# Clustered attention and two feed-forward layers on one core: attention per whole head, W from rounded parts, reloads split in place

## The chip, the core and the metric

One Trainium2 chip, of which the program uses one core. The metric is device time in microseconds (us). The engines are TensorE (PE in the views; its weight loads are PEld), VectorE (DVE), ScalarE (ACT), GpSimd (POOL, idle here but for a few set-up instructions) and SyncE (SP), whose queue issues every DMA of this kernel.

## The reference

```python
q_n, k_n, c_n = normalised q, k, centroids
q_assign = argmax(q_n . c_n); k_assign = argmax(k_n . c_n)   # 16 clusters per head
scores = where(q_assign == k_assign, q @ k.T / 8, -1e9)
attn = exp(scores - max) / (sum + 1e-9);  x = attn @ v        # B=2, H=8, S=768, D=64
x = x as [1536 tokens, 512]
h = x @ w_in                                                  # 512 -> 2048
g = (a0 + a1 h + a2 h^2 + a3 h^3) / (1 + |b0||h| + |b1| h^2 + 1e-6)
y = g @ w_out                                                 # 2048 -> 512
out = ((y @ w1) * (y @ w2)) @ w3 @ w_out2                     # 512 -> 1024 -> 1024 -> 512
```

The weights arrive as 64-bit words, which the kernel decodes to float32 itself.

## The kernel before

**The work.** The 1536 tokens are four chunks of 384 (c = 0 to 3; two per batch). For each chunk there are four stages of matmuls, each of blocks of one 128 x 1024 weight tile: p1 (w_in, 8 blocks, and the rational function on 128 x 768 values behind each), p2 (w_out, 8 blocks), p3 (w1 and w2 together, 8 blocks, and the product of the two), p4 (W, 4 blocks). W is w3 @ w_out2, made once at the start: `FirstW` makes four of its eight row tiles in one go from 16 half blocks, `w_block` one more each for m = 4 to 7.

**Attention.** It goes by chunk: `Attn(c)` works on the 384 queries of a chunk, and per head on three units of 128 queries. A unit is a score matmul (L802), a maximum (DVE, L814), an exponential (ACT, L815), six transposes in two lots (L842) that ScalarE copies out (L845). After two heads `av` multiplies by v (L876). K is rounded and split for the first chunk of a batch, stored to `k_d`, and loaded again for the second chunk.

**Numbers in two parts.** A float32 product is made in one of two ways. A block of kind "D" multiplies plain float32 words (L545). The others split weight and activation each into a rounded part (fp32r, a copy on ScalarE, `hi`) and the rest (a subtraction on VectorE, `lo`), and add three products hi.hi, hi.lo, lo.hi (L547 to L549). In chunk 0 the w_in and w_out blocks are of kind "D" and the w1/w2 blocks of kind "E" (decoded, then split); all are also stored to DRAM as decoded words. Later chunks reload them, kind "S": the load lands in a slot of the class `raw`, is rounded into `hi` (L501) and subtracted into `lo` (L502), two slots of the class `w`. p4 loads both parts of W ready made, kind "L". W itself is made from plain float32 words (L590, L606).

**Order.** All operations are written down as tasks with their operands, and a planner (`Plan`) places them on the four queues by list scheduling with fixed costs, going forward and backward some rounds; the best order is emitted as it stands. Each engine runs its instructions strictly in that order. Buffers are slots of classes (`SLOTS`: six `w`, three `raw`, three `et`, two PSUM slots each of `s` for scores and p1, `t` for transposes and attention output, `m` for the other stages). `CFG` holds the numbers that steer the priorities: in which window of blocks how much attention lies (`AT`), and leads and offsets.

Of the kernel before, what the change touches and what calls it, by code (L numbers as in the profile page):

```python
# [21 lines left out]
    F0=('in', 'out'),  # L22
    KEEP=(),
    NORM=(4, 4, 4, 4),
    NW=(1, 4),
    AT=(1.5, 2.2083, 2.5833, 4.0, 4.0, 4.0, 4.0, 4.0, 4.0),
    M1=1,
    LEAD=(5.9, 35.7, 45.3),
    ALEAD=(23.9, 20.0),
    MLEAD=252.0,  # L30
    AOFF=3.7,
    SLOTS={'w': 6, 'raw': 3, 'y': 3, 'x': 2, 'ab': 4, 'x2': 2, 'g': 16, 'et': 3, 'E': 4, 'kqr': 1, 'A': 2, 'B': 2, 'v': 1, 'sm': 6, 'nn': 3, 's': 2, 't': 2, 'm': 2, 'sums': 2, 'rb': 1},
    WO2=-768.4,
# [254 lines left out]
def kernel(  # L288
# [15 lines left out]
    cfg=CFG,  # L304
# [17 lines left out]
    if not only_plan:  # L322
# [67 lines left out]
    def masks(b, pr):  # L390
# [11 lines left out]
        def one(which, src):  # L402
# [19 lines left out]
            op("ACT", 0.83, lambda: s.activation(two(rn.t), ss.t[:, :, 0:TC], AF.Ln, bias=tiny), [ss], [rn], p0)  # L422
# [3 lines left out]
            op("DVE", 0.87, lambda: w.tensor_tensor(two(u.t), two(rn.t), lg.t[:, :, 0:TC], ALU.mult), [rn, lg], [u], p0)  # L426
# [6 lines left out]
            def count():  # L433
                for hf in range(2):
                    nc.tensor.matmul(cnt.t[:, hf, 0:TC], tri, u.t[:, hf * TC:(hf + 1) * TC])
# [3 lines left out]
                two(v.t), cnt.t[:, :, 0:TC], 0.0, two(u.t), ALU.is_equal, ALU.mult), [cnt, u], [v], p0)  # L439
            if which:  # L440
                op("ACT", 0.74, lambda: s.activation(u.t, v.t, AF.Copy, scale=-BIG), [v], [u], p0)
                dma(lambda: msk_d[b, :, 0:TC], lambda: u.t[:, 0:TC], 196608, [u], [("msk", b, 1)], p0)
                dma(lambda: msk_d[b, :, TC + S:], lambda: u.t[:, TC:], 196608, [u], [("msk", b, 2)], p0)
            else:
                op("ACT", 0.74, lambda: s.activation(u.t, v.t, AF.Identity, bias=one1, scale=-1.0), [v], [u], p0)
                dma(lambda: msk_d[b, :, TC:TC + S], lambda: u.t, 393216, [u], [("msk", b, 0)], p0)
# [26 lines left out]
    class Blk:  # L473
# [7 lines left out]
        def prep(self):  # L481
            k, at = self.kind, self.at
            pl, psp = at - cfg["LEAD"][0 if k != "L" else 1] - (0 if k == "L" else cfg["LEAD"][1]), at - cfg["LEAD"][1]
            if k in "DE":
                self.f = Buf("w", [P, WB])
                raws = [load_raw(self.src, i, at - cfg["LEAD"][2]) for i in range(2)]
                for i in range(2):
                    decode(raws[i], lambda i=i: self.f.t[:, i * HB:(i + 1) * HB], (self.f, i), psp)
                if self.full is not None:
                    dma(lambda: self.full[0](), lambda: self.f.t, 524288, [(self.f, 0), (self.f, 1)], [self.full[1]], at)  # L490
                if k == "D":
                    return
            elif k == "S":
                self.f = Buf("raw", [P, WB])
                dma(lambda: self.f.t, self.full[0], 524288, [self.full[1]], [(self.f, 0), (self.f, 1)], pl)
            self.hi, self.lo = Buf("w", [P, WB], F32R), Buf("w", [P, WB], F32R)
# [3 lines left out]
            else:  # L500
                op("ACT", 0.95, lambda: nc.scalar.copy(self.hi.t, self.f.t), [(self.f, 0), (self.f, 1)], [self.hi], psp)  # L501
# [14 lines left out]
    def moe_blk(c, n, i, src):  # L516
# [3 lines left out]
        if c == 0:  # L520
            if n in F0:
                return Blk("D", src, full)
# [554 lines left out]
```

## Time and profile before

| what | us |
|---|---|
| median of 3 runs (range) | 808.32 (805.76 to 809.25) |
| the profiled execution's own time | 805.77 |
| its span, first to last instruction | 804.0 |
| PE busy in the span | 775.6 (96%) |
| VectorE, ScalarE busy | 614.1 (76%), 555.8 (69%) |

The difference between time and span (1.8 us) lies outside the instructions. Busy time of PE counts a matmul from its start to its modelled end, and neighbours overlap, so the distance from one start to the next tells more than the mean duration does. The same holds, less strongly, for VectorE and ScalarE.

### The profile page before, as it was taken

What the parts mean: (1) busy time and instruction counts of PE and PEld (TensorE: products, weight loads), DVE (VectorE), ACT (ScalarE), POOL (GpSimd) and SP (SyncE); (2) the same over time, 40 slices, a digit from 0 to 9 for tenths busy, and PEclk for the clock granted to TensorE, in tenths of its full rate; (3) what the DMA queues carried; (4) which work ended last, traced back from release to release, by engine and by line L of the source; (5) the groups of instructions that cost most, each with busy time, mean ns of one, the idle gap of its engine ahead of it and who ended that gap; (6) DMA issues with size and microseconds to landing.
All of it is one profiled execution on the core that took longest, in us unless ns stands there. A gap on an engine that the chain in (4) does not pass through costs nothing.

```text
span 804.0 us, 11696 instructions
## 1 busy us (share of the span) xinstructions
PE 775.6 (96%) x4225; PEld 636.7 (79%) x4225; DVE 614.1 (76%) x842; ACT 555.8 (69%) x959; POOL 0.7 (0%) x6
## 2 busy tenths in 40 slices
PE   3998999998999999999999999999999999999998
PEld 1346655565665768888889889899999999999998
DVE  6988887659999987989999663299994399983440
ACT  4887877778797867899898755378763388663331
POOL 0000000000000000000000000000000000000000
PEclk9999999999999999999999999999999999999999
DMA  8998899998768499666777842243557343653324
GB/s 322 367 304 265 272 293 262 294 284 269 233 174 295 135 368 315 206 207 216 224 234 234 286 161 97 87 132 105 206 199 229 105 134 130 228 178 132 132 103 146
DMA packets 67641, 172.08 MB, mean 214 GB/s; under 512 B 7680, under 2 KB 29952, under 8 KB 67584
## 3 DMA queue, kind: packets, MB, share of 16 engines
q1 hardware_dynamic: 67584, 171.34, 65.2%
q8 instruction: 33, 0.54, 0.3%
q14 instruction: 24, 0.20, 0.1%
HBM read 134.88 MB, written 33.29 MB: 209 GB/s over the span
## 4 chain that ended last, share of the span: by engine, by line
PE 81%; DMA 10%; ACT 4%; DVE 3%; issue 1%; SPq 1%; ACTq 0%; DVEq 0%
PE m L547 12%; PE m L548 12%; PE m L549 12%; PE s L802 6%; PE t L842 6%; PE t L876 6%; PE m L545 5%; DMA raw<-in_w_in_dram 4%; PE s L547 4%; PE s L545 4%; PE s L549 4%; PE s L548 4%; PE m L606 2%; PE t L590 1%; DMA raw<-fin 1%
## 5 line engine op out<-in xcount | busy, mean ns | idle before, releaser
L502 DVE TENSOR_TENSOR w<-raw,w 128x1024 fp32r<-128x1024 f32 x72 | 87.9, 1222 | 60.8 <-ACT w L501 55.2
L501 ACT CAST w<-raw 128x1024 fp32r<-128x1024 f32 x72 | 75.8, 1053 | 82.0 <-PE m L548 59.7
L814 DVE TENSOR_REDUCE sm<-s 128x1 f32<-128x768 f32 x96 | 90.7, 951 | 16.9 <-PE s L802 15.9
L845 ACT COPY et<-t 128x384 f32<-128x384 f32 x192 | 87.8, 494 | 21.6 <-PE t L842 19.5
L815 ACT ACTIVATE E<-s,sm 128x768 f32<-128x768 f32 x96 | 88.2, 920 | 12.5 <-DVE sm L814 10.7
L842 PEld LDWEIGHTS t<-ident,E 128*128 128x128 f32 x576 | 68.8, 140 | 34.1 <-issue 12.1
L842 PE MATMUL t<-ident,E 128*128 128x128 f32 x576 | 86.6, 276 | 7.7 <-ACT et L845 4.4
L547 PE MATMUL m<-x,w 128*128 128x384 f32 x256 | 87.4, 341 | 0.0
L548 PE MATMUL m<-x,w 128*128 128x384 f32 x256 | 86.2, 337 | 0.0
L549 PE MATMUL m<-x,w 128*128 128x384 f32 x256 | 86.1, 336 | 0.0
L876 PE MATMUL t<-et,v 128*64 128x384 f32 x384 | 69.0, 494 | 0.0
L547 PE MATMUL s<-x,w 128*128 128x384 f32 x192 | 66.1, 345 | 0.0
L547 PE MATMUL m<-g,w 128*128 128x384 f32 x192 | 64.9, 338 | 0.0
L549 PE MATMUL s<-x,w 128*128 128x384 f32 x192 | 64.9, 338 | 0.0
L549 PE MATMUL m<-g,w 128*128 128x384 f32 x192 | 64.7, 337 | 0.0
L548 PE MATMUL s<-x,w 128*128 128x384 f32 x192 | 64.6, 336 | 0.0
L548 PE MATMUL m<-g,w 128*128 128x384 f32 x192 | 64.6, 336 | 0.0
L802 PE MATMUL s<-A 128*128 128x384 f32 x192 | 60.6, 397 | 2.4 <-ACT E L815 1.8
L466 ACT ACTIVATE y<-raw 128x512 f32<-128x512 f32 x67 | 46.0, 692 | 22.3 <-DMA raw<-in_w_in_dram 9.4
L802 PE MATMUL s<-B 80*128 80x384 f32 x192 | 49.6, 339 | 0.0
L547 PEld LDWEIGHTS m<-x,w 128*128 128x128 f32 x256 | 48.1, 188 | 1.2 <-issue 1.2
L876 PEld LDWEIGHTS t<-et,v 128*64 128x64 f32 x384 | 24.7, 136 | 29.9 <-issue 27.7
(128 smaller groups left out, 1658.3 us busy)
## 6 DMA issues: line engine op xcount, KB each, us to landing
raw<-fin SPq DMA_DIRECT2D x24, 512.0 KB, 3.3
raw<-fout SPq DMA_DIRECT2D x24, 512.0 KB, 3.3
raw<-f SPq DMA_DIRECT2D x24, 512.0 KB, 3.2
kqr<-in_kq_dram SPq DMA_DIRECT2D x16, 576.0 KB, 5.4
raw<-in_w3t_dram SPq DMA_DIRECT2D x16, 512.0 KB, 5.5
raw<-in_w_in_dram SPq DMA_DIRECT2D x16, 512.0 KB, 6.1
raw<-in_w_out_dram SPq DMA_DIRECT2D x16, 512.0 KB, 4.9
raw<-in_w_dram SPq DMA_DIRECT2D x16, 512.0 KB, 5.1
```

The source lines that it names most:

```text
L501: op("ACT", 0.95, lambda: nc.scalar.copy(self.hi.t, self.f.t), [(self.f, 0), (self.f, 1)], [self.hi], psp)
L502: op("DVE", 1.135, lambda: nc.vector.tensor_tensor(self.lo.t, self.f.t, f32(self.hi.t), ALU.subtract), [(self.f, 0), (self.f, 1), self.hi] ...
L545: nc.tensor.matmul(o, w.f.t[:, sl], x[0], start=first, stop=last)
L547: nc.tensor.matmul(o, w.hi.t[:, sl], x[0], start=first, stop=False)
L548: nc.tensor.matmul(o, w.hi.t[:, sl], x[1], start=False, stop=False)
L549: nc.tensor.matmul(o, w.lo.t[:, sl], x[0], start=False, stop=last)
L802: nc.tensor.matmul(p.t[:, f, 0:TC], lhs.t[0:n, q0:q0 + P], lhs.t[0:n, k0:k0 + TC], start=st, stop=not st)
L814: op("DVE", 0.865, lambda: nc.vector.tensor_reduce(mx.t, p.t[:, :, 0:TC], axis=AX.XY, op=ALU.max, negate=True), [p], [mx], OF[1])
L815: op("ACT", 0.88, lambda: nc.scalar.activation(E.t, p.t[:, :, 0:TC], AF.Exp, bias=mx.t, accum_out=sums.t[:, qt, h % 2:h % 2 + 1] if late e ...
L842: nc.tensor.transpose(t.t[:, i * P:(i + 1) * P], e[:, kt * P:(kt + 1) * P], ident)
L845: op("ACT", 0.371, lambda t=t, lot=lot: nc.scalar.copy(et.t[:, 3 * lot:3 * lot + 3, qt * P:(qt + 1) * P], t.t[:, 0:TC].rearrange("p (a b) ...
L876: nc.tensor.matmul(o.t[64 * j:64 * j + 64, 0:TC], v.t[:, kt, j, :], ets[j].t[:, kt, :], start=kt == 0, stop=kt == NKT - 1)
```

## The change

Five things change together. (1) Attention goes by batch and whole head: six units of 128 queries per head, K prepared once in SBUF, no `k_d`. So the 48 units of batch 0 must all be done before p1 of chunk 0 can start, where 24 had to before. (2) x is stored once as float32 and split where p1 loads it, not in `av`. (3) W is made from rounded parts in three products; the 16 half blocks of `FirstW` and the four of `w_block` are split for it. (4) The w_out blocks of chunk 0 are of kind "E" and not "D", and with them g of chunk 0 is split. (5) A reloaded block lands in the slot that becomes `lo`, and the subtraction is done in place. The numbers in `CFG` are others throughout, and so is the order. Two buffers of p1's rational function move from `et` to `raw`.

```diff
-    F0=('in', 'out'),
+    F0=("in",),
+    SPLIT=8,
-    AT=(1.5, 2.2083, 2.5833, 4.0, 4.0, 4.0, 4.0, 4.0, 4.0),
+    AT=(0.0, 1.5, 2.5, 3.5417, 4.0, 4.0, 4.0),
...
         def prep(self):
+            if k != "S":
+                self.f = f = Buf("w", [P, WB])
+            if k != "D":
+                self.lo = Buf("w", [P, WB], F32R)
+            if k == "S":
+                f = self.lo
...
             elif k == "S":
-                self.f = Buf("raw", [P, WB])
-                dma(lambda: self.f.t, self.full[0], 524288, [self.full[1]], [(self.f, 0), (self.f, 1)], pl)
-            self.hi, self.lo = Buf("w", [P, WB], F32R), Buf("w", [P, WB], F32R)
+                dma(lambda: f32(f.t), self.full[0], 524288, [self.full[1]], words, pl)
+            self.hi = Buf("w", [P, WB], F32R)
...
     class FirstW:
+            def split(hi, lo, src, pr):
+                op("ACT", 0.48, lambda: nc.scalar.copy(part(hi), src.t), [src], [hi], pr)
+                op("DVE", 0.6, lambda: nc.vector.tensor_tensor(part(lo), src.t, f32(part(hi)), ALU.subtract), [src, hi], [lo], pr)
...
                         for m in (m0, m0 + 1):
-                            nc.tensor.matmul(o[m].t, self.f[j].t[:, m * P:(m + 1) * P], w2[j][0].t[:, w2[j][1]],
-                                             start=j == 0, stop=j == 7)
+                            mm(o[m].t, self.hi[j].t, self.lo[j].t, m * P, [part(x) for x in w2[j]], j == 0, j == 7)
...
     def w_block(m):
-        blk = Blk("D", lambda: w3t_d[m])
+        blk = Blk("E", lambda: w3t_d[m])
...
     def p1_block(c, mp):
+                if len(xs[c]) > 1:
+                    hi = xs[c][0]
+                    for p in range(NP):
+                        op("ACT", 0.371, lambda p=p: nc.scalar.copy(hi.t[:, p], f32(f.t[:, p])), [(f, p)], [(hi, p)], at - 4)
+                        op("DVE", 0.469, lambda p=p: nc.vector.tensor_tensor(
+                            f.t[:, p], f32(f.t[:, p]), f32(hi.t[:, p]), ALU.subtract), [(hi, p)], [(f, p)], at - 4)
...
     class Attn:
-            if first:
-                dma(lambda: k_d[b, h, 0], lambda: f32(A.t[0:64, ks]), 196608, [(A, "k", 0)], [("k", b, h, 0)], at)
-                dma(lambda: k_d[b, h, 1], lambda: f32(Bt.t[0:64, ks]), 196608, [(Bt, "k")], [("k", b, h, 1)], at)
...
             if x in first:
-                attend(24 * (first[x] + 1))
+                attend(48 * (first[x] // 2 + 1))
```

Three places show how the order moves. First VectorE before the change, where the last operand of `FirstW` is decoded (L467, L468 and L470 are the decode; L429, L430 and L438 the masks; L782 and L785 the preparation of a head):

```order
L429 TENSOR_TENSOR g_376<-g_376,nn_388 128x768
L782 SCALAR_TENSOR_TENSOR A_393<-kqr_356,A_393 64x384
L430 STREAM_TRANSPOSE g_365<-g_376 128x768
L785 TENSOR_TENSOR B_412<-kqr_356,A_393 64x768
L468 SCALAR_TENSOR_TENSOR y_386<-raw_340,y_386 128x512
L470 SCALAR_TENSOR_TENSOR w_428<-raw_340,y_386 128x512
L438 SCALAR_TENSOR_TENSOR g_376<-s_422,g_365 128x768
```

The decode of the last operand is row 75 of its queue, with 66 rows from the first decode ahead of it. After the change the same place reads (L580 is the new split of `FirstW`):

```order
L580 TENSOR_TENSOR w_496<-E_434,w_474 128x512
L580 TENSOR_TENSOR g_508<-E_481,g_492 128x512
L467 TENSOR_SCALAR y_438<-y_438 128x512
L467 TENSOR_SCALAR y_479<-y_479 128x512
L468 SCALAR_TENSOR_TENSOR y_438<-et_368,y_438 128x512
L468 SCALAR_TENSOR_TENSOR y_479<-raw_408,y_479 128x512
L470 SCALAR_TENSOR_TENSOR E_531<-et_368,y_438 128x512
L470 SCALAR_TENSOR_TENSOR E_533<-raw_408,y_479 128x512
L580 TENSOR_TENSOR g_547<-E_531,g_535 128x512
L580 TENSOR_TENSOR w_549<-E_533,w_543 128x512
L797 SCALAR_TENSOR_TENSOR A_551<-kqr_504,A_551 64x2x384
L822 TENSOR_REDUCE sm_566<-s_553 128x1
```

The last split is row 92, with 83 rows ahead of it: 48 of the decode, 16 splits, 12 of two mask passes, 2 of a head, 6 short ones.

Second, TensorE at the end of `FirstW`, before the change (L590 `FirstW`, L435 masks, L802 scores, L842 transposes):

```order
L590 MATMUL t_267<-ab_338,w_428 128x512
L590 MATMUL t_266<-ab_338,w_428 128x512
L435 MATMUL s_522<-g_464,tri 128x384 x2
L802 MATMUL s_534<-A_393 128x384 x2
L802 MATMUL s_534<-B_412 128x384 x2
L802 MATMUL s_545<-A_393 128x384 x2
L802 MATMUL s_545<-B_412 128x384 x2
L842 MATMUL t_559<-ident,E_554 128x128 x3
```

and after it (L540 to L542 are the three products, L814 the scores):

```order
L814 MATMUL s_553<-A_384 128x384 x2
L814 MATMUL s_553<-B_388 128x384 x2
L814 MATMUL s_561<-A_384 128x384 x2
L814 MATMUL s_561<-B_388 128x384 x2
L540 MATMUL t_264<-g_535,w_543 128x512
L541 MATMUL t_264<-g_547,w_543 128x512
L542 MATMUL t_264<-g_535,w_549 128x512
L540 MATMUL t_263<-g_535,w_543 128x512
L541 MATMUL t_263<-g_547,w_543 128x512
L542 MATMUL t_263<-g_535,w_549 128x512
```

The first two score units stand ahead of the last 12 products of `FirstW`, which need the split of row 92. From the start to the end of `FirstW` TensorE has 96 W products, 32 L415 and 4 L435 matmuls and two units (row 1 to 135). Before the change it has, up to the first `w_block` matmul (row 1 to 113), 32 W products, 64 L415 and 8 L435 matmuls, and 16 score matmuls and 12 transposes of the first units.

Third, SP's queue at reloads of w_out late in the program, before the change:

```order
L350 DMA raw_5813<-fout 128x1024 [waits DMAHW6_49,DVE_49]
L350 DMA out_dram<-y_5815 128x384 [waits DMAHW7_49,Activation_49]
L350 DMA raw_5850<-fout 128x1024 [waits DMAHW0_49,DVE_49]
L350 DMA out_dram<-y_5866 128x384 [waits DMAHW1_49,Activation_49]
L350 DMA raw_5895<-fout 128x1024 [waits DMAHW2_49,DVE_49]
```

and after it:

```order
L350 DMA w_6035<-fout 128x1024 [waits DMAHW2_49,PE_49]
L350 DMA w_6040<-fout 128x1024 [waits DMAHW3_49,PE_49]
L350 DMA out_dram<-y_6037 128x384 [waits DMAHW4_49,Activation_49]
L350 DMA w_6068<-fout 128x1024 [waits DMAHW5_49,DVE_49,PE_49]
L350 DMA w_6098<-fout 128x1024 [waits DMAHW6_49,DVE_49,PE_49]
```

A reload waited for VectorE to have read a `raw` slot; now it waits for TensorE to be done with a `w` slot.

## Rows read from the trace of the kernel before

**Rows 1.** The page, parts 1 and 4: busy time; the chain that ended last.

```profile
PE 775.6 (96%) x4225; PEld 636.7 (79%) x4225; DVE 614.1 (76%) x842; ACT 555.8 (69%) x959; POOL 0.7 (0%) x6
...
PE 81%; DMA 10%; ACT 4%; DVE 3%; issue 1%; SPq 1%; ACTq 0%; DVEq 0%
```

**Rows 2.** Stretches: length, busy PE, PEld, DVE, ACT, POOL, clock, DMA share, GB/s.

```profile
20.00:60.00 40.00, 39.31 (x196) 15.34 (x194) 35.95 (x54) 33.71 (x49) 0.00 (x0) 1.00 0.97 336
60.00:170.00 110.00, 102.98 (x534) 66.32 (x534) 86.05 (x132) 84.17 (x182) 0.00 (x0) 0.98 0.92 276
200.00:465.00 265.00, 263.46 (x1418) 205.59 (x1419) 240.25 (x340) 219.77 (x405) 0.00 (x0) 1.00 0.74 240
465.00:801.00 336.00, 335.73 (x1934) 329.07 (x1932) 214.49 (x248) 184.15 (x261) 0.00 (x0) 1.00 0.43 147
```

**Rows 3.** The chain in order of time: start, length, what, number of instructions.

```profile
24.80 1.43 PE s L415 x16
...
115.42 1.72 PE m L606 x4
...
121.98 4.04 PE t L876 x24
...
158.09 0.70 PE t L842 x6
...
250.27 10.32 PE s L545 x32
```

**Rows 4.** Timeline of TensorE at the end: two products, 24 starts apart.

```profile
791.66 0.34 PE L547 MATMUL m<-ab,w 128*128 128x384 f32 x1
...
795.86 0.33 PE L547 MATMUL m<-ab,w 128*128 128x384 f32 x1
```

**Rows 5.** Timeline of TensorE: first W products, first scores, first `w_block`, first p1, first p2 of chunk 1.

```profile
10.72 5.47 PE L590 MATMUL m<-ab,w 128*128 128x512 f32 x8 [10.72 <-DVE ab L470]
...
59.85 0.81 PE L802 MATMUL s<-A 128*128 128x384 f32 x2
...
70.80 1.88 PE L606 MATMUL m<-ab,w 128*128 128x512 f32 x4
...
170.30 1.46 PE L545 MATMUL s<-x,w 128*128 128x384 f32 x4
...
465.43 0.33 PE L547 MATMUL m<-g,w 128*128 128x384 f32 x1
```

**Rows 6.** Timeline of VectorE: first decode, last decode of `FirstW`, four starts in a row.

```profile
6.01 0.43 DVE L467 TENSOR_SCALAR y<-y 128x512 uint32<-128x512 uint32 x1 [3.49 <-ACT y L466]
...
46.86 0.69 DVE L470 SCALAR_TENSOR_TENSOR w<-raw,y 128x512 uint32<-128x512 uint32 x1
...
245.43 0.42 DVE L467 TENSOR_SCALAR y<-y 128x512 uint32<-128x512 uint32 x1
245.77 0.69 DVE L470 SCALAR_TENSOR_TENSOR w<-raw,y 128x512 uint32<-128x512 uint32 x1
246.37 0.95 DVE L658 TENSOR_TENSOR et<-et,s 128x768 f32<-128x768 f32 x1
247.24 0.69 DVE L468 SCALAR_TENSOR_TENSOR y<-raw,y 128x512 uint32<-128x512 uint32 x1
```

**Rows 7.** A stretch in which VectorE is full (columns as in rows 2).

```profile
240.00:280.00 40.00, 40.00 (x174) 25.75 (x173) 39.74 (x57) 31.90 (x56) 0.00 (x0) 1.00 0.68 219
```

**Rows 8.** Two stretches of 2 us around a gap of TensorE (columns as in rows 2).

```profile
64.00:66.00 2.00, 1.18 (x7) 0.87 (x7) 2.00 (x4) 1.36 (x4) 0.00 (x0) 0.88 0.26 94
66.00:68.00 2.00, 2.00 (x6) 1.09 (x5) 1.56 (x3) 0.68 (x3) 0.00 (x0) 0.50 0.36 102
```

**Rows 9.** Reloads: groups of instructions (count, busy us, mean ns, idle before), and the DMA (count, KB, us to landing).

```profile
L502 DVE TENSOR_TENSOR w<-raw,w 128x1024 fp32r<-128x1024 f32 x72 | 87.9, 1222 | 60.8 <-ACT w L501 55.2 <-PE s L548 3.8 <-ACT et L656 1.1
L501 ACT CAST w<-raw 128x1024 fp32r<-128x1024 f32 x72 | 75.8, 1053 | 82.0 <-PE m L548 59.7 <-issue 11.2 <-PE s L548 5.9
...
raw<-fin SPq DMA_DIRECT2D x24, 512.0 KB, 3.3
```

More of the change, by code (lines that the diff above doesn't have):

```diff
@@ L513, in cost @@
         def cost(self, n):
-            return n * (0.646 if self.kind == "D" else 0.489)
+            return n * (0.645 if self.kind == "D" else 0.523)
     def moe_blk(c, n, i, src):
         full = (lambda: f_d[n][i], ("f", n, i))
-        parts = tuple((lambda j=j: s_d[n][j, i], [("s", n, i, j)]) for j in range(2))
-        keep = n in cfg["KEEP"]
         if c == 0:
-            if n in F0:
-                return Blk("D", src, full)
-            return Blk("E", src, None if keep else full, parts if keep else None)
-        if keep:
-            return Blk("S" if c == 1 and n in F0 else "L", None, full, parts)
+            return Blk("D" if n in F0 else "E", src, full)
         return Blk("S", None, full)
@@ L540, in put, with mm, products @@
                src_key + [(dst[0], key)], [(dst[1], key)], pr)
[L542 removed]
+    def mm(o, hi, lo, c0, x, first, last):
         sl = slice(c0, c0 + P)
+        nc.tensor.matmul(o, hi[:, sl], x[0], start=first, stop=False)
+        nc.tensor.matmul(o, hi[:, sl], x[1], start=False, stop=False)
+        nc.tensor.matmul(o, lo[:, sl], x[0], start=False, stop=last)
+    def products(o, w, c0, x, first, last):
         if w.kind == "D":
[L545 to L549 removed]
+            nc.tensor.matmul(o, w.f.t[:, c0:c0 + P], x[0], start=first, stop=last)
+        else:
+            mm(o, w.hi.t, w.lo.t, c0, x, first, last)
     w2 = []
@@ L605, in q @@
                 for j in range(j0, j0 + 2):
-                    nc.tensor.matmul(o.t, blk.f.t[:, j * P:(j + 1) * P], w2[j][0].t[:, w2[j][1]], start=j == 0, stop=j == 7)
+                    mm(o.t, blk.hi.t, blk.lo.t, j * P, [part(x) for x in w2[j]], j == 0, j == 7)
             for j0 in range(0, 8, 2):
-                op("PE", 1.74, lambda j0=j0: q(j0), blk.reads([j0 * P]) + w2[j0:j0 + 2], [o], at)
-            w_out_part(o, m, at)
-        blk.run, blk.pe = run, 6.9
+                op("PE", 1.386, lambda j0=j0: q(j0), blk.reads([j0 * P]) + [k for w in w2[j0:j0 + 2] for k in w], [o], when)
+            w_out_part(o, m, when)
+        blk.run, blk.pe = run, 5.5
         return blk
@@ L826, in unit @@
[L826 to L834 removed]
+            if qt == 0:
+                self.sums[h] = Buf("sums", [P, NQT, 2])
@@ L967, in prep_heads @@
     def prep_heads(i):
-        while state["h"] <= min(i, NCH * H - 1):
-            c, h = divmod(state["h"], H)
-            att[c].prep(h, units[state["h"] * NQT])
+        while state["h"] <= min(i, B * H - 1):
+            b, h = divmod(state["h"], H)
+            att[b].prep(h, units[state["h"] * 2 * NQT])
             state["h"] += 1
@@ L983, in attend @@
                 masks(b, mask_at[b])
-            prep_heads(c * H + h)
-            att[c].unit(h, qt, units[state["u"]])
+            prep_heads(b * H + h)
+            att[b].unit(h, qt, units[state["u"]])
             state["u"] += 1
```

342 lines of the change are left out of this document (151 added, 191 removed).

## The prediction, made before the changed kernel ran

> **What bounds the kernel now.** I read the page first, then stretches, then starts. TensorE is busy for 96% of the span and holds 81% of the chain [rows 1]. Busy time overlaps between neighbours, so I price TensorE by starts: a plain float32 product of 384 columns is two instructions of 10.32/32 = 0.3225 us (I price L435 like it), one of 512 columns takes 2 x 1.72/4 = 0.86, L415 0.089 and L842 0.117 per instruction, an attention-output product (L876) 2 x 4.04/24 = 0.34 [rows 3]; a rounded product of 384 columns takes 4.20/24 = 0.175 [rows 4], and a score matmul the same. The counts are those of the two orders. From 465.43 to 801 the kernel before has 1824 rounded products (319.2) and the rest of four units (15.9): 335.1 of work in 335.6 us. That stage is pure TensorE. Upstream it isn't: the first W product starts at 10.72 after waiting for a decode; at 70.80 TensorE has done 48.4 us of work and is 22.4 behind [rows 5]; from there to 170.30 it does 92.5 in 99.5 (32 W products, 124 scores, 195 transposes, 60 L876), to 465.43 then 286.5 in 295.1 (128 plain and 480 rounded products, 228 scores, 375 transposes, 108 L876). So the early stages lose, and there DMA is at 92% (60 to 170) and VectorE at 91% (200 to 465) [rows 2].
>
> **TensorE's own work.** The w_out blocks of chunk 0 have 64 plain products: 64 x 0.645 = 41.3 becomes 192 x 0.175 = 33.6, -7.7. W has 64 plain products of 512 columns: 64 x 0.86 = 55.0. No row shows a rounded product of 512; by columns from the one of 384 it is an estimate of 0.175 x 512/384 = 0.233, so 192 x 0.233 = 44.8, -10.2. Its bounds are 0.175 (as dear as the shorter one, -21.4 for W) and 0.43 (as dear as half a plain one, +27.6); I take the columns and leave both bounds out of the range, since the plain ones scale just so: 0.43/0.3225 = 512/384. Scores, transposes and attention output keep their counts. Together -17.9.
>
> The Trainium skill ("FP8 and Floating Point Precision", TensorE Precision Notes) says that true FP32 takes four passes through the array; by that three products cost three quarters of one plain one, 0.645 for W, and W would give -13.8 and the sum 3.6 less. Rows 4 show 0.175 and not a quarter of 0.645, so the rounded products have a cost beside their columns, and the sum goes by the rows.
>
> **The start.** The cover of the new splits is missing here, since TensorE waits for its operands. VectorE has, from its first decode to the last split of `FirstW`, 84 instructions in place of 67 to the last decode: 48 of decode (0.34 and twice 0.60 from start to start [rows 6], together 24.6), 16 splits of 512 elements (no row; like the decode's two-input operations of 512, 0.60: 9.6), 12 mask operations and 2 of a head of 768 elements (0.87 [rows 6]: 12.2) and six short ones (1): 47.4. Before it is 36.4 for the same place, reached at 46.86 + 0.6, from a start at 6.01 [rows 6], 5 us later than the work alone. With the same delay the last split ends at 6.0 + 47.4 + 5 = 58.4; the 12 products that stand behind it take 2.8 (0.3 for the handoff), so TensorE has finished `FirstW` at about 61 (56 if VectorE never starves, as it has more to do between arrivals; 64 if it starves twice as long). By then it has done 96 x 0.233 + 32 x 2 x 0.089 + 4 x 0.645 + 8 x 0.175 = 32.1 and is 28.9 behind, 6.5 more than before at the same place. The ScalarE copies for these splits run beside (84% busy there [rows 2]).
>
> **From there to p1.** The order now has 52 units, 96 W products and half of the masks before the first p1 product: 139.2 of work (W 22.4, masks 8.3, 208 scores 36.4, 336 transposes 39.5, 96 L876 32.6). Before it had 31 units and lost 7.0, which is 0.226 per unit; for 52 that is 11.7. DMA gives back some of it: 16 stores and 48 loads of `k_d` parts fall away, and x is stored once, so DMA is not at 92% in this stretch. Nothing shows how much of the 7.0 was DMA; between all (loss 0) and none (11.7, or 17 if ScalarE, with 52 units in the place of 31, costs half as much again) I take 9. p1 starts at 61 + 139.2 + 9 = 209.
>
> **p1 of chunk 0 to p2 of chunk 1.** TensorE has 42 units, 64 plain and 672 rounded products: 254.6 of work (41.3 and 117.6, with 168 scores 29.4, 288 transposes 33.7, 96 L876 32.6) (286.5 before). VectorE has 241 by its starts (before 248.8): 26 splits of 1024 in place of 18, 14 splits of g in place of 7, 42 maxima in place of 55. So VectorE falls by 8 and TensorE by 32; its share of TensorE's work goes from 87% to 95%. Before, 8.6 us were lost here. From 240 to 280 VectorE is busy 39.74 of 40 and TensorE 40.00 [rows 7], so a full VectorE can be lived with when the order suits. I take 8.6 x 254.6/286.5 = 7.6 and 3.5 for tightness (bounds 0 and 25, worked out below as a rival). p2 of chunk 1 starts at 209.2 + 254.6 + 11.1 = 474.9.
>
> **From there to the end.** The same 1824 products, 319.2, and no unit left. The tail behind the last product is 3.0 (801 to 804). The reloads in place: 1222 + 1053 ns for the two operations and 3.3 for the DMA [rows 9] make 5.6, with three handoffs of 0.2 to 0.3 some 6.3. Before, the DMA landed in `raw` ahead of time, and ScalarE waited 59.7 us in all for a `w` slot [rows 9]. Now the DMA itself waits for that slot. Six slots are three blocks, so a freed slot is wanted again two blocks on, 2 x 24 x 0.175 = 8.4 us. That covers 6.3 with 2 to spare; without cover a late operation costs its delay. I add 1. Splitting x in p1 is 4 short operations of VectorE per chunk, while it is busy 214 of 336 us [rows 2], and costs nothing; without that cover 4 x 0.5 per chunk.
>
> **Sum.** 474.9 + 319.2 + 1 + 3.0 = 798.1 us of span, -5.9: TensorE's work -17.9, whereof the worse start takes 6.5, the units 2, VectorE's tightness 2.5, the reloads 1. The profiled execution has 1.8 beside its span and is 2.5 under the median, so 798.1 + 4.3 = 802 for the median.
>
> **Rivals.** (a) The start costs nothing and DMA's relief is whole: -17.9 and no losses added gives 786 + 4.3 = 790. For it: DMA at 97% in 20 to 60 [rows 2] may be what bounds the start, and it has no more to bring than before. Against it: 47.4 us of VectorE work lie ahead of the last product. (b) It ends slower: VectorE becomes the bound from p1 of chunk 0 to p2 of chunk 1. Before, its work by starts filled 84% of that stretch (248.8 of 295.1). If it can't do better, 241 takes 286 and not 265.7: +20, 822. It decides when the stretch takes 276 us (+10, past 812), a share of 87%. For it: maxima, splits and the rational function queue in one order, and a late maximum stops scores, with two PSUM slots. Against it: rows 7. (c) Reloads come late: half a microsecond for each of the 56 blocks or so behind the attention gives +28, 830; it needs the spare 2 us to go, by queueing on ScalarE and VectorE in p3 and p1. Against it: in p2 and p4 both have hardly anything else to do. (d) The clock. TensorE was busy for 1.18 of 2 us in 64 to 66, and the granted clock was 0.50 in 66 to 68, which is 1.2 GHz of the 2.4 [rows 8]; it will have gaps all through the start. If it ran at 1.2 GHz throughout, its 32.1 us of work there would take 64, ending at 75 and not at 61: +14, 816. Against it: before, the clock was 1.00 from 20 to 60 [rows 2], behind a start that had waited to 10.72 [rows 5].
>
> By the Trainium skill ("TensorE: Matmul & The Clock Gate", Part 1) the throttled state is the default and activity lifts it; rows 8 agree, and this would make (d) more likely than I hold it to be.
>
> **How the numbers follow.** The forecast as summed (796 to 808): 0.55. (a) 0.18. (b) 0.12, (c) 0.08, (d) 0.07. Half a per cent (804.3 to 812.4) is about what a measurement here can tell. The forecast's own range lies in faster for two thirds and in same for one; (a) is faster; the slower cases reach into same with a quarter. Faster 0.37 + 0.18 = 0.55, same 0.18 + 0.07 = 0.25, slower 0.20. The range takes in (a) to 787 and the partial forms of (b) and (d) to 818.
>
> **What would show it.** TensorE's last product of `FirstW` at about 61; first p1 product near 209; first p2 product of chunk 1 near 475, then 319 us without idle time. W products of 512 columns 0.233 apart. If p1 starts later than 215, the units are the cause; if the stretch to p2 takes over 271 with VectorE full, (b) in part or whole; if TensorE is idle behind 475 with ScalarE waiting for a reload, (c); a clock below 1 before 60, (d). The forecast is wrong in kind if one of these stretches loses more than the 18 us saved.

## The result, and the profile after

The changed kernel takes 812.78 us (median of 8 runs, 810.60 to 816.58), the kernel before 807.52 (8 runs beside it): a measured ratio of 1.0062, 95% interval 1.0041 to 1.0082. It is 0.6% slower. The profiled execution is the slowest of the eight (816.58, mean granted clock 0.989; the other seven show 0.993 to 0.996), so its span of 814.8 is 10.8 above that of before, where the medians differ by 5.3: half of the 10.8 belongs to these two executions. Five executions of 1058 to 2663 us (four of three kernels in the table below, one of the kernel before) are left out of all medians and ratios.

The page after the change, parts 1 and 4 [rows 1]:

```profile
PE 772.4 (95%) x4353; PEld 663.7 (81%) x4353; DVE 638.0 (78%) x862; ACT 578.8 (71%) x979; POOL 0.7 (0%) x6
...
PE 74%; ACT 13%; DMA 5%; DVE 5%; issue 2%; SPq 1%; DVEq 0%; ACTq 0%
```

ScalarE's share of the chain went from 4% to 13%, TensorE's from 81% to 74%. Stretches, with columns as in [rows 2]: to the last product of `FirstW`, ten microseconds out of that, on to the first p1 product, from there to p2 of chunk 1, and the stage behind.

```profile
0.00:62.50 62.50, 39.92 (x176) 25.63 (x177) 53.49 (x97) 46.25 (x74) 0.70 (x6) 0.92 0.84 299
35.00:45.00 10.00, 2.04 (x5) 0.97 (x4) 9.96 (x16) 7.88 (x12) 0.00 (x0) 0.68 0.91 316
62.50:223.40 160.90, 151.64 (x906) 106.80 (x904) 123.68 (x180) 133.25 (x281) 0.00 (x0) 0.98 0.65 205
223.40:492.00 268.60, 261.45 (x1448) 212.24 (x1449) 247.91 (x339) 224.50 (x389) 0.00 (x0) 1.00 0.52 174
492.00:811.40 319.40, 319.40 (x1826) 319.07 (x1824) 212.89 (x248) 174.33 (x236) 0.00 (x0) 1.00 0.44 153
```

From 35 to 45 VectorE is full (9.96 of 10) and TensorE hardly works (2.04 of 10). In the kernel before, VectorE is as full at that time, and TensorE busy throughout:

```profile
35.00:45.00 10.00, 10.00 (x50) 3.84 (x49) 9.94 (x16) 8.54 (x13) 0.00 (x0) 1.00 1.00 375
```

The timeline of TensorE after the change, which answers to [rows 4, 5], says for what it waits:

```profile
11.81 0.79 PE L540 MATMUL m<-x,w 128*128 128x512 f32 x1 [11.81 <-ACT w L579]
...
43.42 2.93 PE L435 MATMUL s<-g,tri 128*128 128x384 f32 x4 [7.96 <-DVE g L430]
...
47.43 0.63 PE L540 MATMUL m<-x,w 128*128 128x512 f32 x1
47.85 0.63 PE L541 MATMUL m<-x,w 128*128 128x512 f32 x1
...
57.19 0.39 PE L540 MATMUL m<-g,w 128*128 128x512 f32 x1
57.42 0.40 PE L541 MATMUL m<-g,w 128*128 128x512 f32 x1
...
62.53 0.39 PE L542 MATMUL m<-g,w 128*128 128x512 f32 x1
...
223.42 0.91 PE L546 MATMUL s<-x,w 128*128 128x384 f32 x2 [0.34 <-ACT E L823]
```

It waits 7.96 us for a mask operation (L430) that stands in VectorE's queue between decodes and splits:

```profile
41.79 0.68 DVE L580 TENSOR_TENSOR x<-E,x 128x512 fp32r<-128x512 f32 x1
42.39 0.97 DVE L430 STREAM_TRANSPOSE g<-g 128x768 f32<-128x768 f32 x1
43.29 0.39 DVE L467 TENSOR_SCALAR y<-y 128x512 uint32<-128x512 uint32 x1
43.59 0.68 DVE L580 TENSOR_TENSOR w<-E,w 128x512 fp32r<-128x512 f32 x1
```

During the wait VectorE starts six mask operations, three of the decode and one split; nine splits, some 5.4 us, stand ahead of L430 since the start. A product of 512 columns starts 0.23 us after the one before (57.19 to 57.42), and 0.42 behind that wait (47.43 to 47.85), where the granted clock was 0.50.

**An account by stretches.** I price TensorE's work up to a place in its order as the prediction does (a rounded product of 512 columns at the measured 0.2315) and take it from the time at which TensorE gets there. "Behind" is that difference at the end of `FirstW`; the other two columns are what is lost from there to the first p1 product, and from p1 to the last product. Each row is one profiled execution; us is the median. The ratio is to executions of before that ran beside each kernel, so it differs by up to 0.2% from the quotient of two medians.

| kernel | us | ratio (95%) | behind, `FirstW` | lost to p1 | lost after p1 |
|---|---|---|---|---|---|
| before | 807.5 | 1 | 17.4 (at 59.0) | 12.1 | 8.3 |
| changed | 812.8 | 1.0062 (1.0041 to 1.0082) | 30.9 (62.9) | 21.7 | 14.2 |
| b_w_parts | 813.0 | 1.0082 (1.0056 to 1.0108) | 23.6 (58.5) | 21.6 | 9.8 |
| b_wout_parts | 814.0 | 1.0089 (1.0069 to 1.0109) | 17.5 (59.8) | 17.6 | 18.4 |
| b_in_place | 807.5 | 1.0005 (0.9989 to 1.0020) | 14.7 (57.6) | 9.8 | 14.3 |
| b_parts_345 | 822.7 | 1.0184 (1.0161 to 1.0207) | 22.7 (54.8) | 23.9 | 24.1 |
| b_fitted | 802.8 | 0.9947 (0.9924 to 0.9969) | 15.2 (59.5) | 10.0 | 11.2 |
| b_parts_fitted | 815.3 | 1.0095 (1.0061 to 1.0129) | 26.2 (64.5) | 17.0 | 23.3 |
| a_attn_only | 811.7 | 1.0053 (1.0033 to 1.0073) | 17.7 (53.6) | 11.2 | 15.7 |
| a_w_plain | 807.9 | 0.9993 (0.9980 to 1.0007) | 18.4 (54.3) | 13.9 | 14.5 |
| b_first_parts | 816.2 | 1.0094 (1.0055 to 1.0133) | 24.9 (61.2) | 16.3 | 13.8 |
| a_first_parts | 811.7 | 1.0033 (1.0002 to 1.0065) | 29.2 (61.2) | 12.0 | 15.7 |
| a_no_lo | 808.7 | 1.0012 (0.9991 to 1.0033) | 26.9 (58.9) | 16.5 | 16.9 |
| a_pool_split | 829.7 | 1.0265 (1.0243 to 1.0287) | 38.8 (70.8) | 16.2 | 27.7 |
| a_copy_dve | 818.1 | 1.0121 (1.0099 to 1.0144) | 28.5 (60.5) | 17.5 | 20.8 |
| b_48_units | 813.2 | 1.0054 (1.0034 to 1.0074) | 15.8 (60.1) | 24.8 | 8.4 |

For the change: TensorE's work 763.0 to 744.7, -18.3; behind at `FirstW` +13.5; lost to p1 +9.6; after p1 +5.9; together +10.7 of the 10.8. (A median close to that of before can hide in a profiled run some us above it, so I read only differences of 5 us and more, and those that several kernels share.)

### The profile page after: what moved, and what is told of

The parts are those of the page before. It is cut to its first block, busy times and chain, and to the rows that moved or that the text cites. A ratio compares the mean times of both kernels' runs of the same rounds, so it can differ in the third digit from the quotient of the medians.

```text
span 814.8 us, 11761 instructions
## 1 busy us (share of the span) xinstructions
PE 772.4 (95%) x4353; PEld 663.7 (81%) x4353; DVE 638.0 (78%) x862; ACT 578.8 (71%) x979; POOL 0.7 (0%) x6
## 4 chain that ended last, share of the span: by engine, by line
PE 74%; ACT 13%; DMA 5%; DVE 5%; issue 2%; SPq 1%; DVEq 0%; ACTq 0%
PE m L540 14%; PE m L542 14%; PE m L541 14%; PE t L872 6%; PE s L814 4%; PE s L540 4%; PE s L542 4%; PE s L541 4%; ACT E L823 4%; PE t L836 4%; PE s L546 3%; ACT et L839 3%; DMA wld<-raw 2%; DMA whd<-w 1%; DMA g<-in_kt_dram 1%
## 5 line engine op out<-in xcount | busy, mean ns | idle before, releaser
L507 DVE TENSOR_TENSOR w<-w,w 128x1024 fp32r<-128x1024 f32 x92 | 111.6, 1222 | 67.3 <-ACT w L506 61.8
L506 ACT CAST w<-w 128x1024 fp32r<-128x1024 f32 x92 | 96.3, 1054 | 84.1 <-PE m L541 63.6
L540 PE MATMUL m<-g,w 128*128 128x384 f32 (+1 forms) x396 | 135.9, 343 | 0.0
L541 PE MATMUL m<-g,w 128*128 128x384 f32 (+1 forms) x396 | 134.2, 339 | 0.0
L542 PE MATMUL m<-g,w 128*128 128x384 f32 (+1 forms) x396 | 134.1, 339 | 0.0
L540 PE MATMUL m<-x,w 128*128 128x384 f32 (+1 forms) x292 | 104.4, 358 | 12.6 <-ACT w L579 12.6
L839 ACT COPY et<-t 128x384 f32<-128x384 f32 x192 | 89.3, 503 | 21.7 <-PE t L836 20.0
L542 PE MATMUL m<-x,w 128*128 128x384 f32 (+1 forms) x292 | 102.6, 351 | 0.3 <-DVE w L580 0.3
L541 PE MATMUL m<-x,w 128*128 128x384 f32 (+1 forms) x292 | 102.4, 351 | 0.0
L836 PE MATMUL t<-ident,E 128*128 128x128 f32 x576 | 88.3, 279 | 7.7 <-ACT et L839 4.2
L540 PEld LDWEIGHTS m<-g,w 128*128 128x128 f32 x396 | 74.3, 188 | 1.6 <-issue 1.2
L542 PEld LDWEIGHTS m<-g,w 128*128 128x128 f32 x396 | 74.3, 188 | 0.5
L541 PEld LDWEIGHTS m<-g,w 128*128 128x128 f32 x396 | 74.4, 188 | 0.4
L540 PEld LDWEIGHTS m<-x,w 128*128 128x128 f32 x292 | 56.0, 192 | 15.2 <-ACT w L579 13.4
L540 PE MATMUL s<-x,w 128*128 128x384 f32 x192 | 65.4, 341 | 0.3 <-ACT E L823 0.3
L542 PE MATMUL s<-x,w 128*128 128x384 f32 x192 | 64.6, 336 | 0.0
L814 PE MATMUL s<-A 128*128 128x384 f32 x192 | 57.9, 383 | 6.6 <-ACT E L823 6.1
```

The costliest lines, as they stand in the source:

```text
L506: op("ACT", 0.95, lambda: nc.scalar.copy(self.hi.t, f32(f.t)), words, [self.hi], psp)
L507: op("DVE", 1.135, lambda: nc.vector.tensor_tensor(self.lo.t, f32(f.t), f32(self.hi.t), ALU.subtract), words + [self.hi], [self.lo], psp)
L540: nc.tensor.matmul(o, hi[:, sl], x[0], start=first, stop=False)
L541: nc.tensor.matmul(o, hi[:, sl], x[1], start=False, stop=False)
L542: nc.tensor.matmul(o, lo[:, sl], x[0], start=False, stop=last)
L814: nc.tensor.matmul(p.t[:, f, 0:TA], lhs.t[0:n, q0:q0 + P], lhs.t[0:n, k0:k0 + TA], start=st, stop=not st)
```

## Experiments

**The parts alone, in the kernel before.** Part (3) alone (b_w_parts), part (4) alone (b_wout_parts), part (5) alone (b_in_place), all three (b_parts_345); attention and the numbers of the order are those of before. A kernel with part (3) also names places for the parts of w_out2.

```diff
 # b_w_parts: splits, products and w_block as in the change, and
+    W2=(("ab", "ab", "ab"), ("x", "x", "g", "g")),
 # b_wout_parts
-    F0=('in', 'out'),
+    F0=('in',),
 # b_in_place
-                self.f = Buf("raw", [P, WB])
+                self.f = self.lo = Buf("w", [P, WB], F32R)
```

> The kernel before, with part (3) alone: W from rounded parts, the operands of FirstW and of the w_block blocks split for it; attention by chunk stays, and all numbers that steer the order. Theory A (whole-head attention puts 48 units ahead of p1, they are paced by ScalarE, and the work saved on TensorE is lost there; the parts themselves gain): W saves 10.2 of TensorE and the later start of FirstW costs 4 to 6, so 3 to 6 us faster than before, about 803. Theory B (the splits at the start eat what they save, whatever the attention): FirstW ends at 60 or later with TensorE 30 behind, 8 more than before; with the w_block part (-5.1) and the FirstW part (-5.1) it comes out between 2 faster and 4 slower.

> The kernel before, with part (4) alone: the w_out blocks of chunk 0 and g of chunk 0 in rounded parts. Theory A: 64 x 0.645 becomes 192 x 0.175 on TensorE, -7.7, about 800. Theory C (VectorE is the bound from p1 of chunk 0 to p2 of chunk 1): 8 more splits of 1024 (1.2 each) and 8 of g (0.87) bring some 16 us more to a VectorE that is 91% busy there, so nothing is gained, or up to 8 us lost: 808 to 816.

> The kernel before, with part (5) alone: a reloaded block lands in the slot that becomes lo. Theory A and B: within 2 us of before, since a freed slot is wanted again 8.4 us later and a reload needs 6.3. Theory D (reloads come late while VectorE and ScalarE are full, in the middle stage): more than 3 us slower, with TensorE waiting for L501 or L502 between 200 and 465, and no idle time of TensorE behind that.

> The kernel before, with parts (3), (4) and (5) together: what is left of the change is attention by whole head, x stored once, and the numbers that steer the order. Theory A: -10.2 + 5 for the start and -7.7: 12 us faster, about 796, and the changed kernel's 812.8 is then the price of whole-head attention and its order. Theories B, C, D: the parts cost their gain by themselves: 806 to 816, about as the changed kernel.

Theory A fell at once. W from parts costs 0.8% and w_out from parts 0.9% with attention by chunk; together 1.8%. Only the reloads in place cost nothing. The parts came out dearer than their own theories had them: W some 6 us slower where B allowed 4, and all three 822.7 where B, C and D allowed 806 to 816. In b_w_parts the first p1 product comes at 175.5 (before 170.3), although TensorE has 10.6 us less to do up to there; its stretches are:

```profile
0.00:58.50 58.50, 41.55 (x221) 24.17 (x225) 52.38 (x98) 47.86 (x75) 0.70 (x6) 0.97 0.85 303
...
58.50:175.50 117.00, 105.10 (x588) 75.64 (x589) 95.30 (x141) 93.25 (x196) 0.00 (x0) 0.96 0.92 279
```

**Other numbers for the order, and whole-head attention alone.** Numbers chosen for one kernel may not suit another, so these three had theirs chosen anew (`LEAD`, `AT`, `OFF` and the like): before with parts (3) to (5), the changed kernel without them, and before with nothing else.

```diff
 # b_fitted: CFG (not shown), and the planner's costs as in the changed kernel
-            return n * (0.646 if self.kind == "D" else 0.489)
+            return n * (0.645 if self.kind == "D" else 0.523)
-            op("PE", 0.654, smm, [(A, "q0"), (A, "q1"), (A, "k", 0), (A, "k", 1), (Bt, "m"), (Bt, "k"), (Bt, "q")], [p], OF[0])
+            op("PE", 0.71, smm, [(A, "q0"), (A, "q1"), (A, "k", 0), (A, "k", 1), (Bt, "m"), (Bt, "k"), (Bt, "q")], [p], OF[0])
...
 # a_attn_only: CFG, W from plain words, and
+    F0=('in', 'out'),
+                f = Buf("raw", [P, WB])
```

> The kernel before with parts (3), (4) and (5), as b_parts_345, but with the numbers that steer the order, and the planner's cost of a product, chosen anew for it. Theory N (the 15 us that b_parts_345 lost were mostly numbers that did not fit): 804 to 811. Theory P (the parts cost more than they save, whatever the numbers): 813 to 822. With attention by chunk and the parts on both sides it is also the partner of the changed kernel: the difference to 812.8 is whole-head attention.

> The changed kernel with parts (3), (4) and (5) undone, numbers of the order chosen for it: attention by whole head and x stored once alone. Theory Q (whole-head attention by itself costs, since 48 units must stand ahead of p1): 812 to 822, slower than before, with 10 us or more lost between FirstW and p1. Rival P (whole-head attention gains by its smaller traffic and the parts took that away): below 805.

> The kernel before with nothing but the numbers that steer the order, and the planner's costs of products and scores, chosen anew. If the numbers alone are worth several us, this is 798 to 804; if the kernel before was at what its order can give, 805 to 810. It is the measure of what a difference between two kernels with different numbers may owe to the numbers.

The numbers alone are worth 0.5% (b_fitted), and this is the fastest kernel here, 1.2% under the changed one (802.78/812.78). With numbers of their own the parts still cost 0.95% against before, and 1.5% against b_fitted, the same kernel without them (theory P, not N). Whole-head attention alone is 1.0053 against 0.9947 for the kernel before in the same comparison: it costs too, 1.1%, but not where theory Q says. 53 units stand ahead of its p1, and it loses 11.2 us there, where before loses 12.1 with 35. Against b_fitted it loses 2.5 more at the start, 1.2 more to p1 and 4.5 more after p1, none of them over the 5 us that I read. With the parts on both sides whole-head attention costs nothing that can be told (812.8 against 815.3 for b_parts_fitted). x stored once, part (2), came with it and was not tried alone.

```profile
53.60:208.50 154.90, 148.76 (x867) 98.36 (x865) 119.83 (x176) 129.40 (x276) 0.00 (x0) 1.00 0.69 213
```

ScalarE is as full there (129.40 of 154.90, 84%) as in the changed kernel (133.25 of 160.90, 83%), and the loss is half: ScalarE's load alone does not make it.

**Part (3) undone, whole and by half.** a_w_plain makes W from plain words; a_first_parts and b_first_parts keep the parts in `FirstW` and make the `w_block` products plain.

```diff
 # a_w_plain (numbers chosen anew)
-                            mm(o[m].t, self.hi[j].t, self.lo[j].t, m * P, [part(x) for x in w2[j]], j == 0, j == 7)
+                            nc.tensor.matmul(o[m].t, self.f[j].t[:, m * P:(m + 1) * P], part(w2[j]), start=j == 0, stop=j == 7)
 # all three
-        blk = Blk("E", lambda: w3t_d[m])
+        blk = Blk("D", lambda: w3t_d[m])
```

> The changed kernel with part (3) undone: W from plain float32 words, no splits in FirstW and w_block. The numbers that steer the order had to be others, since the changed kernel's don't fit the other buffers, so a part of a difference may be theirs. Theory P (what stands ahead of p1 is not paced by TensorE; the splits lengthen it and the shorter products don't shorten it, as in the kernel before with part (3) alone, which was 6 us slower): TensorE has 10.2 us more work and the kernel is yet 2 to 7 us faster than the changed one, 806 to 811, with TensorE less than 28 behind at the end of FirstW. Rival R (TensorE's work counts everywhere, and whole-head attention is what lost): 5 to 10 slower than the changed kernel, 818 to 823.

> The kernel before with half of part (3): FirstW from rounded parts, the four w_block blocks in plain products, with the numbers of before (the plain products of w_block multiply by the rounded part of w_out2 alone, so those rows of W are not the reference's). In b_w_parts the stretch from FirstW to p1 lost 21.6 us of TensorE's time, before 12.1. Theory W (the loss there is the w_block blocks' own: shorter products beside the units and four more splits of 1024 on ScalarE and VectorE): 10 to 14 lost there, the start 6 further behind as in b_w_parts, 810 to 813. Rival F (it is the late start that is handed on, whatever w_block does): 18 to 23 lost there, 815 to 820.

> The changed kernel with half of part (3) undone: FirstW from rounded parts, the four w_block blocks in plain products by the rounded part of w_out2 (those rows of W are not the reference's); numbers of the order chosen anew. The stretch from FirstW to p1 lost 21.7 us in the changed kernel and 13.9 with the whole of part (3) undone. Theory W: 12 to 16 lost there, with 5 us more of TensorE's work. Rival F: 19 to 24 lost there, and the time 815 to 820.

Theory P holds by its range: with 10.6 us more work for TensorE, a_w_plain is 0.7% faster than the changed kernel (0.9993 against 1.0062) and level with before. Its numbers were chosen anew and the changed kernel with numbers chosen anew was not run, so these 5 us could be the numbers; but that the parts of W cost shows without that in b_w_parts, with the numbers of before. From 35 to 45, and from `FirstW` to p1, it shows

```profile
35.00:45.00 10.00, 9.71 (x23) 3.93 (x22) 9.85 (x18) 4.32 (x8) 0.00 (x0) 1.00 1.00 324
54.30:212.00 157.70, 151.52 (x868) 99.16 (x866) 121.57 (x178) 130.09 (x277) 0.00 (x0) 0.99 0.68 212
```

From 35 to 45 VectorE is as full as in the changed kernel, but TensorE is fed. The start divides the kernels cleanly: 14.7 to 18.4 behind in the seven with a plain `FirstW`, 22.7 to 38.8 in the nine with a rounded one. But 5.3 us of that come by the way of counting, when `FirstW` with less work ends no earlier. With attention by chunk and the numbers of before it does just that (59.0 before, 58.5 in b_w_parts, 54.8 and 61.2 in the other two): the splits cost there about what the products save. With whole heads it ends 7 to 9 later with rounded parts (62.9 and 61.2) than with plain words (53.6 and 54.3).

The stretch to p1 divides less well. The changed kernel fits theory W (12.0 lost with plain `w_block`, 21.7 with parts). But 3.4 of the 21.7 lie in a stretch at half clock (below, rival (d)) that a_first_parts does not have, and the medians of the two differ by 1.0 us, with intervals that overlap: the parts of `w_block`, 5.3 us less work, bring no time. In the kernel before the same half gives 16.3, between W and F, and its time fell in F's range. b_wout_parts and b_48_units, both with plain W, lose 17.6 and 24.8 there. So the `w_block` parts are a cause of the loss to p1 in the changed kernel, and not the only one.

**What paces the start.** a_no_lo leaves the 16 subtractions out, a_pool_split gives them to GpSimd.

```diff
 # a_no_lo (numbers chosen anew)
-                op("DVE", 0.6, lambda: nc.vector.tensor_tensor(part(lo), src.t, f32(part(hi)), ALU.subtract), [src, hi], [lo], pr)
...
-                w2.append((hi, lo))
+                w2.append((hi, hi))
 # a_pool_split
-                op("DVE", 0.6, lambda: nc.vector.tensor_tensor(part(lo), src.t, f32(part(hi)), ALU.subtract), [src, hi], [lo], pr)
+                op("POOL", 1.2, lambda: nc.gpsimd.tensor_tensor(part(lo), src.t, f32(part(hi)), ALU.subtract), [src, hi], [lo], pr)
```

> The changed kernel without the 16 subtractions of FirstW's splits on VectorE; hi stands in the place of lo, so W is not the reference's, while the products of TensorE and the copies of ScalarE stay as many. Numbers of the order chosen anew. Theory V (VectorE paces the start; the subtractions are 9.6 us of it): the last product of FirstW at 52 to 57 and the granted clock at 1.00 from 35 to 50, and the kernel at 803 to 809. Rival D (transfers or ScalarE pace the start): the last product at 60 to 63, the time at 811 to 814. Rival B (the start does not reach the end, since what stands behind it waits for something else): the last product at 52 to 57, p1 yet at 221 to 224 and the time at 811 to 814.

> The changed kernel with the 16 subtractions of FirstW's splits on GpSimd, which is idle, in place of VectorE. Theory V (VectorE paces the start; it is busy for 40.5 of 42.8 us there): the 9.6 us that fall away bring the last product of FirstW forward from 62.5 to 54 to 59, if one subtraction takes GpSimd less than 1.5 us, and the kernel gains 3 to 6, 807 to 810. Rival D (the transfers pace the start): the last product stays at 61 to 63 and the time at 811 to 814. Rival G (GpSimd takes over 2 us for one, or slows VectorE beside it): the last product comes later than 64 and the kernel is slower.

Without the subtractions `FirstW` ends 4.0 earlier, p1 starts 9.9 earlier and the kernel is 4.1 us faster: theory V in kind, though `FirstW` comes at 58.9 and not by 57. TensorE works through the place where it stood:

```profile
0.00:58.90 58.90, 38.55 (x177) 23.95 (x177) 41.52 (x79) 44.05 (x70) 0.70 (x6) 0.97 0.90 318
35.00:45.00 10.00, 8.24 (x34) 5.83 (x33) 9.39 (x17) 6.75 (x11) 0.00 (x0) 1.00 0.93 303
```

VectorE now has 41.52 us of work in 58.90, so it no longer paces all of the start. With whole heads and plain words `FirstW` ended some 9 us earlier than in the changed kernel, and 4.0 of these go with the subtractions; the copies on ScalarE and the order of the rest were not tried apart. The run also has numbers of its own, and its `FirstW` holds one buffer of class `w` per operand where the changed kernel's holds two. That was hardly what held the changed kernel: ScalarE waited 0.7 us in all for TensorE to leave such a slot (L579, up to 75). On GpSimd the subtractions made it worse, `FirstW` at 70.8 (rival G). Two groups of its trace, then the two of the changed kernel that answer to the second (instructions by line and shape: count, busy us, mean ns):

```profile
L581 POOL TENSOR_TENSOR w<-E,w 128x512 fp32r<-128x512 f32 x8 | 14.3, 1786 | 12.8 <-ACT w L580 10.5 <-issue 2.3
...
L468 DVE TENSOR_SCALAR y<-y 128x512 uint32<-128x512 uint32 x15 | 10.2, 683 | 1.7 <-ACT y L467 1.7
L471 DVE SCALAR_TENSOR_TENSOR E<-raw,y 128x512 uint32<-128x512 uint32 x10 | 8.8, 885 | 0.1
```

```profile
L470 DVE SCALAR_TENSOR_TENSOR E<-raw,y 128x512 uint32<-128x512 uint32 x10 | 6.8, 684 | 0.1
L467 DVE TENSOR_SCALAR y<-y 128x512 uint32<-128x512 uint32 x15 | 6.1, 412 | 1.6 <-ACT y L466 1.4
```

One subtraction of this group took GpSimd 1.8 us on average, and the mean of VectorE's own decodes in that time rose from 0.41 to 0.68 and from 0.68 to 0.89.

**What paces the units ahead of p1.** a_copy_dve moves one of two copies of each unit of batch 0 from ScalarE to VectorE; b_48_units puts 11 more units ahead of p1 in the kernel before (46 for 35; the 42 and 31 below count from the first `w_block` product).

```diff
 # a_copy_dve
+                if lot and self.b == 0:
+                    op("DVE", 0.469, lambda t=t, lot=lot: nc.vector.tensor_copy(
+                        et.t[:, 3 * lot:3 * lot + 3, i * P:(i + 1) * P], t.t[:, 0:TA].rearrange("p (a b) -> p a b", a=3)),
+                        [t], [(et, lot, i)], OF[4])
+                    continue
 # b_48_units
-    AT=(1.5, 2.2083, 2.5833, 4.0, 4.0, 4.0, 4.0, 4.0, 4.0),
+    AT=(2.0, 2.2083, 2.5833, 4.0, 4.0, 4.0, 4.0, 4.0, 4.0),
```

> The changed kernel with the second of the two copies of each unit of batch 0 (et from PSUM, 0.38 us on ScalarE) on VectorE. Theory S (ScalarE paces the units ahead of p1: 0.88 and twice 0.38 = 1.64 per unit against 1.40 of TensorE without the attention output): p1 starts at 212 to 218 and not at 223.4, and the kernel gains 4 to 9, 804 to 809. Rival L (the units are held up by the chain of handoffs, score, maximum, exponential, transposes, copy, with two slots each, not by ScalarE's load): p1 stays at 221 to 226, and VectorE, 92% busy behind p1, makes the whole 2 to 6 slower.

> The kernel before, with one number of its order changed (AT begins with 2.0 in place of 1.5), by which 42 units of attention stand ahead of the first p1 product in place of 31. Theory Q (units ahead of p1 cost 0.23 to 0.41 us each, because little else stands beside them, and that is the price of whole-head order): p1 starts 11 units later, with 3 to 5 us more lost ahead of it, and the kernel is 2 to 5 us slower, 810 to 813. Rival P (the order of the units alone costs nothing): 806 to 809.

```profile
60.50:215.10 154.60, 144.52 (x892) 101.98 (x890) 144.27 (x227) 115.56 (x229) 0.00 (x0) 1.00 0.67 212
215.10:811.50 596.40, 586.52 (x3285) 536.67 (x3285) 461.72 (x589) 400.24 (x631) 0.00 (x0) 0.99 0.49 161
```

In a_copy_dve p1 starts at 215.1, in the range of theory S, while the time is in that of rival L; 2.4 of the 8.3 come from an earlier `FirstW`, and the loss to p1 falls only from 21.7 to 17.5 while ScalarE goes from 83% to 75%. After p1 it loses 6.6 more, and the kernel is 5.3 slower than the changed one (818.05 against 812.78). So ScalarE may be a part of that loss (4.2 us are under the 5 that I read), and moving its work to VectorE does not pay. In b_48_units 11 more units cost 12.7 us ahead of p1 in a profiled run 3.9 above its median, and 5.0 in the medians: theory Q by its time. But a_attn_only has more units ahead of p1 and no such loss, so their number alone does not set what they cost. That their place in the order does is likely, but not shown: its attention differs too.

## Why the prediction was wrong

**TensorE's own work** was right: -18.3 against -17.9. The product of 512 columns came out at 0.231 (estimate 0.233). By the page of the Trainium skill that the prediction names ("FP8 and Floating Point Precision", TensorE Precision Notes), three products would be, as an estimate, three quarters of 0.86, 0.645; three times 0.231 is 0.69, so the measured products are dearer than that rule has them.

**The start** was right in time and wrong in its comparison. `FirstW` ended at 62.9 (61, range 56 to 64), 30.9 behind (28.9). But the step "6.5 more than before at the same place" did not compare the same place: before's 22.4 belongs to 70.80, the first `w_block` product, and at the end of `FirstW`, at 59.0, it was 17.4 behind. The start cost 13.5: `FirstW` ended 3.9 later with 9.6 less work done, 5.3 of it the saving of rounded products (32 times 0.86 - 3 x 0.2315), the rest for the most part masks moved behind it. The cause, by a_w_plain, a_no_lo and the windows from 35 to 45: the splits join VectorE's queue, which was full already, and TensorE waits. How much of the 13.5 that is was not taken apart beyond the 4.0 of a_no_lo.

**"From there to p1" is the step that failed most**: 9 us of loss, measured 21.7; p1 at 223.4 for 209. Of the 16.7 us between the forecast span (798.1) and the measured one these are 12.7; the start adds 2.0 and the stretch behind p1 2.9. Three things were wrong in it. The base was again counted from 70.80: from the end of `FirstW` before loses 12.1 and not 7.0. The loss was taken as one per unit; a_attn_only loses 11.2 over 53 units, so it isn't. (By that rule and the right base, 12.1 over 35 units, 52 units would lose 18.0, close to what was measured; that would have been luck.) And the parts of `w_block` were costed at their gain of 5.3 alone, where TensorE did not set the pace; with them plain the same stretch loses 12.0. A further 3.4 of the 21.7 are the clock, under rival (d). The relief of DMA that was counted on came (0.92 to 0.65 [rows 2]) and gave nothing back that these runs show. "If p1 starts later than 215, the units are the cause" was wrong as a reading: a_attn_only, with as many units, has p1 at 208.5, so the rest is W and its order.

**Behind p1.** From p1 to p2 of chunk 1 it took 268.6 for 254.6 of work, a loss of 14.0 against 11.1, with VectorE busy for 92%. That is under the 271 us that were to show rival (b), and a full VectorE does not explain the loss: in a_attn_only the same stage loses about as much, with VectorE busy for 84%.

```profile
208.50:488.30 279.80, 271.67 (x1398) 206.73 (x1399) 234.71 (x324) 209.38 (x372) 0.00 (x0) 0.99 0.52 172
```

Part (4), which saves 7.7 in this stage, loses 10 more after p1 than before with attention by chunk (18.4 against 8.3). An estimate of 4 to 5 of these 10, the work that TensorE did at half clock from 226 to 230 and from 281 to 288, is the clock; before has no such stretch there. With whole-head attention parts (4) and (5) gain 3.8 us (a_w_plain against a_attn_only), so half of part (4) may arrive; both have numbers of their own. Why the two differ was not tried; VectorE has 42 maxima there in place of 55.

**To the end** all was right: 319.4 us for 319.2 of work, no idle time. Reloads in place cost nothing (b_in_place 1.0005), the 1 us added for them was not needed, and rival (c) is out. The three handoffs of 0.2 to 0.3 in its reckoning stand in no row: in the trace before, an instruction starts 0.02 to 0.05 us (medians) after the end of what releases it.

**Rival (d)** held in part. The granted clock was 0.50 from 40 to 45, 1.2 of 2.4 GHz, behind a stretch in which TensorE had worked for 0.46 of 5 us. At this clock L435 took 2.93 us for the 1.53 of its other pass, and six products from 45.57 to 48.71 took 3.14 for 1.39: about 3 us. It fell again on the way to p1, behind a stretch in which TensorE waited for copies of ScalarE:

```profile
83.00:86.00 3.00, 1.28 (x10) 0.79 (x8) 1.96 (x3) 3.00 (x7) 0.00 (x0) 1.00 0.98 342
87.00:93.00 6.00, 6.00 (x20) 5.22 (x21) 4.48 (x8) 3.64 (x8) 0.00 (x0) 0.50 0.33 106
```

There W products start 0.42 to 0.43 apart, and the 6.8 us from 86.5 to 93.3 hold 3.4 of work. Before has one such stretch, from 65.5 to 68.9, in which it loses 1.5. So some 5 of the 10.8 between the two profiled executions are the clock, and the other seven executions, with a mean of 0.993 to 0.996, lose less by it. That the Trainium skill ("TensorE: Matmul & The Clock Gate", Part 1) calls the throttled state the default agrees with these rows.

In sum the change saves 18.3 us of TensorE's time, of which 10.6 lie ahead of p1, where TensorE is not what the rest waits for. The splits that buy them cost more than that in the runs with parts of W. What whole-head attention by itself costs lies for the larger part after p1 (15.7 against 11.2), as far as one profiled execution of each can say, and is not explained. Differences between kernels with other numbers carry the 5 us that numbers are worth.

## What to carry to other kernels

Work saved on the busiest engine counts only in the stretches where that engine sets the pace, and such a stretch is known by its lack of idle time, not by the average; price the saving and what it adds to the other queues stretch by stretch. When a loss is carried over from a trace, take both ends at the same place in the program. Compare orders only with numbers chosen for each: choosing them anew for the old kernel gave 0.5%, more than any part of this change is shown to give.

## What the runs showed of the hardware

Some of VectorE's operations grew longer while GpSimd subtracted (a_pool_split): nine of the decode's shifts that lay beside a subtraction for over half of their time took 0.87 us on average, eight others 0.41; of two comparisons in the masks (L430 there, 768 elements, both inputs in SBUF) the one beside a subtraction took 2.04, the other 0.94. Others did not change: a product with one input in PSUM (L427) took 0.94 beside a subtraction and 0.95 without. GpSimd needed 1.3 to 1.8 us (means of three groups) for a subtraction of 512 elements that VectorE does in 0.69. An idle GpSimd was no free helper here.

TensorE's granted clock fell to 0.50 in the middle of the kernel, behind stretches in which it had little to do, and the work that came next took nearly twice as long: products of 512 columns 0.42 to 0.43 us apart in place of 0.23.
